# A four-layer Fourier and sliding-window attention kernel: pairs of visits regrouped, whid products spread over the rounds, twelve norms moved to the second spectral half

## The chip, the core and the metric

The kernel runs on one core of a Trainium2 chip. The metric is the time of one execution on the device in microseconds (us). The engines are PE (TensorE, matmuls and transposes), DVE (VectorE), ACT (ScalarE), POOL (GpSimd) and SP (SyncE), which here only issues DMAs. Each engine takes its instructions in order; what it waits for is a semaphore of another engine or of a DMA.

## What is computed

Four layers run one behind the other on x of 2048 rows and 640 columns. Layers 1 and 3 are Fourier mixing, layers 2 and 4 attention with 32 heads of 20 columns, in which a row sees itself and the 255 rows before it:

```python
def A(x):                      # dft matrices are inputs
    a = einsum("bsd,ed->bse", x, dft_hid_re)
    b = einsum("bsd,ed->bse", x, dft_hid_im)
    return einsum("ts,bse->bte", dft_seq_re, a) - einsum("ts,bse->bte", dft_seq_im, b)
def B(x):                      # H = 32, Dh = 20, W = 256
    q, k, v = heads(x @ wqkv)
    p = softmax(where(0 <= i - j < W, q @ k.T * Dh ** -0.5, -1e9))
    return rows(p @ v) @ wo
x = x + A(layernorm(x)); x = x + B(layernorm(x))
x = x + A(layernorm(x)); x = x + B(layernorm(x))
```

All is float32 to the outside.

## The kernel before

Numbers are split into two float16 parts, high and low, and a product is three matmuls: high by high, high by low, low by high. The program is four functions in a row: `spectral(0)`, `attention(0)`, `spectral(1)`, `attention(1)`.

**A spectral half.** The 16 row tiles of 128 rows are taken in four rounds of four tiles. For each tile, `Hidden.stage` multiplies the normed and transposed tile by the hidden DFT matrix (called whid here): four products of 15 matmuls of 320 columns. ACT and DVE drain each product from its bank of PSUM (lines 265 and 268) and make the seven operands `zc` of a Strassen-like scheme; a bank `f` is one of two. A round then takes eight steps j; a step makes seven sequence products of 12 matmuls each (`main_a`, `main_b`, `main_c`), for two output tiles. Its operands `cc` come from a block of the sequence DFT matrix: POOL makes four sums `cs` (lines 489 to 492), ACT the high parts (497), DVE the low parts (500). DVE adds the results to `res` or `pf` (523), POOL some of them on. Calls of `tick` give out the low parts and the steps of side work: the norm of a coming tile (`side_norm`), the transposes of a tile (`turn_x`), in the first half also the maxima and the splitting of wqkv. The whid products of the next round stand so: tiles 0 and 1 of the round behind steps 6 and 7 of the round before, tiles 2 and 3 between the rounds. In this part a scheduler orders each engine from the program's order.

In `spectral(1)` the tiles come normed, split and transposed out of DRAM: `attention(0)` norms its output tiles (`next_norm`), stores them as `xud`, and `Hidden.fetch` loads them with a transposing DMA.

**An attention half.** The order on each engine is that of the program. It runs over visits G. A visit takes four heads at one row tile; two visits, for the two row tiles of a block of 256 rows, make a pair n. A visit makes the scores of its heads (tiles `st`, first half), DVE masks them and takes row maxima (lines 1061, 1062); after the second visit of a pair the maxima are written as two float16 rows, `tops` (1068, 1069). `hand` transposes them on PE (`hand_on`) and ACT copies them into the operand of the scores (1083, two copies). Visits later `by_key` makes the scores again by key with the maximum subtracted, ACT takes the exponential (1110), POOL masks (1114, 1116), `values` multiplies by v, `back` turns the result and divides. The lags in visits are the constants `HAND_LAG`, `KEY_LAG`, `VALUE_LAG` and `BACK_LAG`. Each visit also runs a unit of other products (`run_unit`: 15 matmuls of q, k, v, of the output or of the next whid stage), and in some even visits a second. DVE's and ACT's own side work, norms and the splitting of wo, runs as `slow_step`, two steps per visit. The products, `values`, `back` and `hand` share the two banks `f`; line 346 drains a product of q or k.

All loads and stores go through SP's queue in order.

## Time and profile before

| | us |
|---|---|
| median of three runs | 2261.99 (2258.68 to 2270.58) |
| profiled execution, its own time | 2264.98 |
| its span | 2263.2 |
| PE busy | 2082.2 (92% of the span) |
| DVE, ACT, POOL busy | 1655.2, 1243.3, 1387.2 |
| mean granted clock of PE | 0.988 |

A busy share is of the whole span; the stages differ. On the trace, spectral 0 runs from 0 to about 593 us (the first scores of attention 0), attention 0 to about 1192, spectral 1 to about 1700, attention 1 to the end. Line 118 is the helper that issues every matmul, so PE's rows are told apart by their tiles. A wait stands as "who, line <- releaser, line: us in total, times, longest".

### The profile page before, as it was taken

What the parts mean: (1) busy time and instruction counts of PE and PEld (TensorE: products, weight loads), DVE (VectorE), ACT (ScalarE), POOL (GpSimd) and SP (SyncE); (2) the same over time, 40 slices, a digit from 0 to 9 for tenths busy, and PEclk for the clock granted to TensorE, in tenths of its full rate; (3) what the DMA queues carried; (4) which work ended last, traced back from release to release, by engine and by line L of the source; (5) the groups of instructions that cost most, each with busy time, mean ns of one, the idle gap of its engine ahead of it and who ended that gap; (6) DMA issues with size and microseconds to landing.
All of it is one profiled execution on the core that took longest, in us unless ns stands there. A gap on an engine that the chain in (4) does not pass through costs nothing.

```text
span 2263.2 us, 54344 instructions
## 1 busy us (share of the span) xinstructions
PE 2082.2 (92%) x21529; PEld 1484.5 (66%) x21529; DVE 1655.2 (73%) x3509; ACT 1243.3 (55%) x2087; POOL 1387.2 (61%) x1788
## 2 busy tenths in 40 slices
PE   7989899899889899999799999999998899999998
PEld 5767566667566666666556777777675666666665
DVE  7887858766668887887767758485857777777774
ACT  5434455344466767676554433433435677676764
POOL 5775968758355665556456858585764555556542
PEclk9999999999999999999899999999999999999999
DMA  6664636454534534354525546363743533443332
GB/s 248 224 213 141 231 133 221 159 197 162 133 86 98 119 85 95 83 113 97 150 83 177 180 138 209 108 210 119 278 137 85 108 81 80 106 96 80 83 78 54
DMA packets 274516, 309.96 MB, mean 137 GB/s; under 512 B 102868, under 2 KB 209620, under 8 KB 264916
## 3 DMA queue, kind: packets, MB, share of 16 engines
q1 hardware_dynamic: 273684, 305.82, 46.8%
q8 instruction: 169, 2.77, 0.5%
q14 instruction: 87, 0.71, 0.1%
q10 hardware_dynamic: 576, 0.66, 0.1%
HBM read 197.26 MB, written 86.87 MB: 126 GB/s over the span
## 4 chain that ended last, share of the span: by engine, by line
PE 43%; DVE 19%; ACT 9%; issue 5%; DMA 4%; POOL 1%; SPq 1%; DVEq 0%; ACTq 0%; POOLq 0%
PE pf L118 22%; PE y L118 7%; DVE m L1062 6%; PE z L118 5%; PE x L118 4%; PE st L118 4%; ACT ptq L1110 4%; ACT qs L1083 3%; DVE st L1061 3%; DVE tops L1069 1%; DVE cc L500 1%; DVE tops L1068 1%; DVE lnt L143 1%; DVE lnst L131 1%; DMA res<-accd 1%
## 5 line engine op out<-in xcount | busy, mean ns | idle before, releaser
L118 PEld LDWEIGHTS <-cc 128*128 128x128 f16 x5376 | 525.4, 98 | 213.3 <-issue 11.4
L1110 ACT ACTIVATE ptq<-st,shift,alpha 128x768 f32<-128x768 f32 (+2 forms) x512 | 474.2, 949 | 147.1 <-POOL ptq L1114 52.6
L118 PEld LDWEIGHTS <-big 128*128 128x128 f16 x4320 | 419.5, 99 | 177.3 <-issue 71.4
L1062 DVE TENSOR_REDUCE m<-st 128x2 f32<-128x512 f32 (+1 forms) x512 | 342.9, 671 | 8.8
L1061 DVE COPY_PREDICATED st<-mask,st 128x256 f32<-128x256 int32 x448 | 191.1, 427 | 184.0 <-PE st L118 145.5
L118 PE MATMUL pf<-early,big 128*128 128x256 f16 x2400 | 291.0, 274 | 18.5 <-ACT qs L1083 7.4
L497 ACT ACTIVATE cc<-cs 128x512 f16<-128x512 f32 x256 | 151.6, 623 | 254.6 <-POOL cs L489 125.4
L118 PE MATMUL y<-zc,cc 128*128 128x320 f16 x1728 | 263.8, 300 | 2.4 <-DVE pf L523 2.4
L500 DVE SCALAR_TENSOR_TENSOR cc<-cs,cc 128x512 f16<-128x512 f32 x256 | 254.3, 1009 | 12.9 <-ACT cc L497 12.7
L118 PE MATMUL pf<-big 128*128 128x320 f16 x1680 | 242.7, 304 | 22.3 <-DVE zc L268 9.6
L1114 POOL TENSOR_SCALAR_AFFINE_SELECT ptq<-ptq 128x512 f32<-128x512 f32 x224 | 144.8, 646 | 134.8 <-ACT ptq L1110 134.2
L1161 POOL CAST os<-o 128x160 f16<-128x160 f32 x128 | 40.5, 316 | 278.1 <-DVE o L1159 278.1
L1116 POOL TENSOR_SCALAR_AFFINE_SELECT ptq<-ptq 128x512 f32<-128x512 f32 x256 | 162.9, 636 | 59.6 <-ACT ptq L1110 59.6
L500 DVE SCALAR_TENSOR_TENSOR cc<-cq,cc 128x512 f16<-128x512 f32 x192 | 194.3, 1012 | 0.0
L118 PE MATMUL pf<-ptq,v 128*32 128x128 f32 (+1 forms) x3840 | 187.5, 335 | 1.4 <-POOL ptq L1116 1.4
L118 PE MATMUL z<-zc,cc 128*128 128x320 f16 x1152 | 177.8, 299 | 3.6 <-DVE res L523 3.6
L118 PE MATMUL x<-zc,cc 128*128 128x320 f16 x1152 | 179.4, 299 | 0.0
L118 PE MATMUL st<-ks,qs 62*128 62x128 f16 (+1 forms) x2016 | 133.1, 236 | 36.2 <-ACT ptq L1110 21.7
L1083 ACT ACTIVATE qs<-pf 2x512 f16<-2x512 f16 x224 | 130.7, 583 | 56.7 <-PE pf L118 54.1
L118 PEld LDWEIGHTS pf<-ptq,v 128*32 128x32 f32 x3840 | 108.2, 111 | 59.8 <-POOL ptq L1116 4.1
L118 PE MATMUL pf<-big,early 128*128 128x320 f16 x960 | 141.1, 299 | 5.9 <-ACT qs L1083 3.2
L118 PEld LDWEIGHTS <-qs 62*128 62x128 f16 x2016 | 82.1, 94 | 83.1 <-issue 64.6
(136 smaller groups left out, 3485.4 us busy)
## 6 DMA issues: line engine op xcount, KB each, us to landing
cq<-in_cmat_dram SPq DMA_DIRECT2D x64, 1024.0 KB
accd<-res SPq DMA_DIRECT2D x96, 320.0 KB
res<-accd SPq DMA_DIRECT2D x96, 320.0 KB
x<-x2d SPq DMA_DIRECT2D x64, 320.0 KB
qkd<-early SPq DMA_DIRECT2D x160, 128.0 KB
ks<-qkd SPq DMA_DIRECT2D x108, 160.0 KB
qs<-qkd SPq DMA_DIRECT2D x84, 160.0 KB
x2d<-res SPq DMA_DIRECT2D x32, 320.0 KB
```

The costliest lines, as they stand in the source:

```text
L118: i = getattr(nc.tensor, what)(*args, **kw)
L131: nc.vector.bn_stats(st[:, h], x[:, h * 320:(h + 1) * 320])
L143: ts(u, g, g, h, op0=OP.mult, op1=OP.mult)
L497: nc.scalar.activation(cc[m][:, 0], f, AF.Copy, scale=C_UP)
L500: nc.vector.scalar_tensor_tensor(cc[m][:, 1], f, C_UP, cc[m][:, 0], op0=OP.mult, op1=OP.subtract)
L1061: nc.vector.copy_predicated(sp[:, :, 2 * P:3 * P], mask[:, None, :].to_broadcast([P, 2, P]), far)
L1062: topped[0] = nc.vector.tensor_reduce(TOP[n][:, 2 * k:2 * k + 2, pi], sp[:, :, c0:3 * P], axis=AX.X, op=OP.max).ins
L1083: nc.scalar.activation(o, handed[n][rs].rearrange("r (i p) t -> r i p t", i=2), AF.Copy)
L1110: nc.scalar.activation(o[:, pi], tps[pi][:, :, first * P:3 * P], AF.Sigmoid, bias=shift, scale=alpha[:, 0:1])
L1114: nc.gpsimd.affine_select(out=q[:, :, a0], in_=q[:, :, a0], pattern=[[0, 4], [-1, P]], base=0, channel_multiplier=1, compare_op=OP.is_gt, ...
L1116: ins = nc.gpsimd.affine_select(out=q[:, :, a0 + 2], in_=q[:, :, a0 + 2], pattern=[[0, 4], [1, P]], base=0, channel_multiplier=-1, compare ...
L1161: nc.gpsimd.tensor_copy(hi, o)
```

## The change

- **Pairs of visits.** The four lags rise by one. The tops of a pair are still written in its second, odd visit; `hand` now runs in the even visit behind it, inside that visit's unit, after eight of its 15 matmuls (`HAND_AT`). `values` falls into the even visit too, `back` into the odd one, and the second unit is taken in odd visits. There is one more visit in all.
- **Side work of attention.** One step in odd visits, two in even ones; two lists, of which the second (`idle`: splitting of wo, norms for the next layer) is served when the first is empty. Rows for the next blocks are loaded two visits earlier and normed three visits earlier.
- **Norms.** Only tiles 0 to 3 of layer three are normed in `attention(0)`. The other twelve are normed in `spectral(1)` as in `spectral(0)`, with the scaling on ACT, and transposed by DMA from SBUF.
- **Whid products.** The table `STAGES` places the four tiles of the next round behind steps 2, 4, 5, 6 in round 0 and 1, 3, 5, 6 in rounds 1 and 2; nothing stands between the rounds. `zc` gets six buffers instead of four; the room comes from a third row of `pf` that is dropped (`p1` is overwritten instead of a new `u3`) and from a smaller area for DMA descriptors.
- **Residuals.** In the last round those of step 7 are loaded ahead of the first stacks of attention. The splitting of wo uses the buffers `res1` instead of `res0`.

```diff
-HAND_LAG = 1
-KEY_LAG = 3
-VALUE_LAG = 5
-BACK_LAG = 6
+HAND_LAG = 2
+KEY_LAG = 4
+VALUE_LAG = 6
+BACK_LAG = 7
+HAND_AT = 8
-NORM_STEPS = (4, 10)
+NORM_STEPS = (0, 4)
+STAGES = ((2, 4, 5, 6), (1, 3, 5, 6), (1, 3, 5, 6))
...
+                    if not first:
+                        turn_load(xt, xs.rearrange("p a b -> p (a b)"))
+                        yield 1
+                        return
...
-                add(u3, z, p1)
-                nc.gpsimd.tensor_tensor(x1[:, hi], x1[:, hi], u3, op=OP.add)
+                add(p1, z, p1)
+                nc.gpsimd.tensor_tensor(x1[:, hi], x1[:, hi], p1, op=OP.add)
...
+            def starts(k):
+                return [max(NJ * r + STAGES[r][k] - 3, k) for r in range(NR - 1)]
...
-                for k in range(0 if r == 0 else 2, RS):
+                for k in range(RS if r == 0 else 0):
...
                         for _ in early_qk:
                             pass
+                        RES[r, j] = load_res(r, j)
...
-                    if first:
-                        if r < NR - 1 and j in (3, 4):
-                            side.append(side_norm(RS * (r + 1) + j - 3))
-                        if r < NR - 1 and j == 5:
-                            turn_x(RS * (r + 1))
+                    for k in range(RS):
+                        if n in starts(k):
+                            side.append(side_norm(RS * (starts(k).index(n) + 1) + k))
+                    if r < NR - 1 and j == STAGES[r][0] - 1:
+                        turn_x(RS * (r + 1), 4 if first else 2)
...
-                    if r < NR - 1 and j >= NJ - 2:
-                        k = j - (NJ - 2)
+                    if r < NR - 1 and j in STAGES[r]:
+                        k = STAGES[r].index(j)
                         s = RS * (r + 1) + k
-                        if first:
-                            turned_x(s)
-                            turn_x(s + 1, 2 if k == 0 else 0)
-                            side.append(side_norm(s + 2))
-                        else:
-                            hidden.fetch(s)
+                        turned_x(s)
+                        if k < RS - 1:
+                            turn_x(s + 1, 2)
                         z_stage(s)
...
-                slow.append(next_norm(i, x3))
+                if i < RS:
+                    idle.append(next_norm(i, x3))
+                else:
+                    done[i, 2] = now[0]
...
-            def run_unit():
+            def run_unit(amid=None):
                 n = 0
                 while n < 15:
+                    if n >= HAND_AT and amid:
+                        amid()
+                        amid = None
...
-                for _ in range(2):
+                for _ in range(1 if G % 2 else 2):
                     slow_step()
...
-                if kept is not None:
-                    hand(kept)
-                    kept = None
                 credit[0] += 2 * max(rate, 400)
-                filled = run_unit()
-                if filled and credit[0] > SECOND and G % 2 == 0:
+                n = due(G, HAND_LAG)
+                run_unit(None if n is None else partial(hand, n))
+                if credit[0] > SECOND and G % 2:
                     run_unit()
-                n = due(G, HAND_LAG)
-                if n is not None:
-                    if filled:
-                        hand(n)
-                    else:
-                        kept = n
```

On PE in the middle of attention 0, from `values` (the `ptq,v` rows) over a unit (`early,big`) and the transposes of the maxima (`idh,tops`) to the next scores (`st<-ks,qs`); "..." leaves out more of the same pairs. Before:

```order
L118 MATMUL pf<-ptq,v 32x128 x4
L118 LDWEIGHTS big
L118 MATMUL pf<-early,big 128x256
...
L118 LDWEIGHTS tops_78
L118 MATMUL pf<-idh,tops_78 66x128
...
L118 LDWEIGHTS qs
L118 MATMUL st_6966<-ks,qs 128x256
```

and with the change:

```order
L120 MATMUL pf<-ptq,v 32x128 x4
L120 LDWEIGHTS big
L120 MATMUL pf<-early,big 128x256
...
L120 LDWEIGHTS tops_78
L120 MATMUL pf<-idh,tops_78 66x128
...
L120 LDWEIGHTS big
L120 MATMUL pf<-early,big 128x256
...
L120 LDWEIGHTS qs
L120 MATMUL st_6966<-ks,qs 128x128
```

The transposes moved from the end of the unit into it, and one visit further from the maxima they read.

On DVE in the first steps of spectral 1 (`cc` rows are low parts, `pf` and `res` rows the additions), before:

```order
L523 SCALAR_TENSOR_TENSOR pf<-y,pf 128x320
L500 SCALAR_TENSOR_TENSOR cc<-cq,cc 128x512
L523 SCALAR_TENSOR_TENSOR res<-x,res 128x320
L500 SCALAR_TENSOR_TENSOR cc<-cq,cc 128x512
L523 SCALAR_TENSOR_TENSOR res<-z,res 128x320
L500 SCALAR_TENSOR_TENSOR cc<-cs,cc 128x512
L523 SCALAR_TENSOR_TENSOR pf<-y,pf 128x320
L500 SCALAR_TENSOR_TENSOR cc<-cs,cc 128x512 x2
L523 SCALAR_TENSOR_TENSOR res<-z,res 128x320
```

and with the change:

```order
L529 SCALAR_TENSOR_TENSOR res<-z,res 128x320
L506 SCALAR_TENSOR_TENSOR cc<-cs,cc 128x512
L133 BN_STATS lnst<-xin 128x6
L529 SCALAR_TENSOR_TENSOR pf<-y,pf 128x320
L506 SCALAR_TENSOR_TENSOR cc<-cs,cc 128x512
L133 BN_STATS lnst<-xin 128x6
L506 SCALAR_TENSOR_TENSOR cc<-cs,cc 128x512
L136 BN_AGGR lnmv<-lnst 128x2
L142 TENSOR_SCALAR lnt<-lnmv 128x1
L143 TENSOR_SCALAR lnt<-lnt 128x1
L145 TENSOR_SCALAR lnt<-lnt 128x1
L146 TENSOR_SCALAR lnt<-lnt 128x1
```

The instructions of a tile's norm (statistics, then short scalars) stand between the low parts and the additions, where none stood.

On SP at the end of spectral 0, around the first stacks `ks` of attention and the residuals of the last step, tiles 125 and 126. Before:

```order
L178 DMA x2d_90<-res 128x640
L178 DMA ks<-onesd_165 2x4096
L178 DMA ks<-qkd_1_148 20x16x256 x6
L178 DMA ks<-onesd_164 2x4096 x2
L178 DMA ks<-qkd_0_147 20x16x256 x6
L178 DMA res<-accd_125 128x640
L178 DMA res<-accd_126 128x640
```

and with the change:

```order
L180 DMA x2d_90<-res 128x640
L180 DMA res<-accd_125 128x640
L180 DMA ks<-onesd_165 2x4096
L180 DMA res<-accd_126 128x640
L180 DMA ks<-qkd_1_148 20x16x256 x6
L180 DMA ks<-onesd_164 2x4096 x2
L180 DMA ks<-qkd_0_147 20x16x256 x6
```

The two residual loads moved ahead of nearly all of the stack loads.

More of the change, by code (lines that the diff above doesn't have):

```diff
@@ L886, in out_tile @@
                     yield from next_layer(i, x3)
-            slow, later = deque(), []
+            slow, idle, later = deque(), deque(), []
             def new_xs():
@@ L912, in split_wo @@
             def split_wo():
-                fs = [keep.tile([P, D], F32, tag="res0", name="wst", bufs=2) for n in range(2)]
+                fs = [keep.tile([P, D], F32, tag="res1", name="wst", bufs=2) for n in range(2)]
                 for n in range(2):
@@ L1195, in slow_step @@
                 with tc.issue_after(topped[0]):
-                    while slow:
-                        try:
-                            return next(slow[0])
-                        except StopIteration:
-                            slow.popleft()
+                    for line in (slow, idle):
+                        while line:
+                            try:
+                                return next(line[0])
+                            except StopIteration:
+                                line.popleft()
             queue_v(0)
@@ L1207, in attention @@
             if layer == 0:
-                slow.append(split_wo())
+                idle.append(split_wo())
             def due(G, lag):
```

21 lines of the change are left out of this document (13 added, 8 removed).

## Prediction

> **What bounds the kernel now.** I read the page's busy shares first, then the busy time by stretch, then who PE (TensorE) waits for in each stretch, and last the timeline at the longest waits. The page:
>
> ```profile
> PE 2082.2 (92%) x21529; PEld 1484.5 (66%) x21529; DVE 1655.2 (73%) x3509; ACT 1243.3 (55%) x2087; POOL 1387.2 (61%) x1788
> ```
>
> By stretch: spectral 0 without its start, the middle of attention 0, spectral 1, the middle of attention 1 (columns: window, length, busy us of PE, PEld, DVE, ACT, POOL with counts, granted clock, DMA share, GB/s):
>
> ```profile
> 120.00:600.00 480.00, 443.49 (x3293) 317.75 (x3291) 346.27 (x642) 210.11 (x400) 338.30 (x292) 0.98 0.55 180
> 600.00:1100.00 500.00, 448.12 (x6046) 319.45 (x6048) 390.38 (x963) 346.50 (x524) 277.66 (x504) 0.99 0.42 97
> 1185.00:1590.00 405.00, 401.58 (x2949) 288.02 (x2949) 278.67 (x454) 166.07 (x339) 282.30 (x233) 1.00 0.50 164
> 1700.00:2190.00 490.00, 450.12 (x6107) 322.43 (x6104) 362.40 (x861) 338.61 (x513) 263.45 (x495) 1.00 0.40 88
> ```
>
> PE bounds every stretch, and the change leaves its instructions as many as they were: 35475 rows in both programs. So only PE's idle time and its clock can give anything. Idle are 36.5, 51.9, 3.4 and 39.9 us in the four; spectral 1 has nothing left to gain. What PE waits for (us in total, times, longest), in spectral 0:
>
> ```profile
> PE pf L118 <- DVE zc L268: 8.3, 4, 5.3
> PE pf L118 <- DVE early L268: 8.2, 2, 6.2
> PE pf L118 <- POOL xs L170: 7.3, 4, 3.2
> PE pf L118 <- DVE big L268: 3.5, 1, 3.5
> ```
>
> in the middle of attention 0:
>
> ```profile
> PE pf L118 <- DVE tops L1069: 15.8, 15, 3.8
> PE pf L118 <- ACT qf L346: 6.6, 11, 0.8
> PE pf L118 <- ACT qs L1083: 6.1, 16, 0.6
> PE st L118 <- DVE m L1062: 2.9, 15, 0.2
> PE pf L118 <- ACT ks L1083: 2.3, 5, 0.5
> ```
>
> and in the middle of attention 1:
>
> ```profile
> PE pf L118 <- DVE tops L1069: 7.3, 12, 1.2
> PE pf L118 <- ACT qs L1083: 6.3, 21, 0.6
> PE pf L118 <- ACT qf L346: 5.8, 10, 0.8
> PE pf L118 <- ACT ks L1083: 2.3, 5, 0.5
> ```
>
> L268 drains a whid product's bank; L1069 and L1083 are the two halves of handing the score maxima on.
>
> **Part 1: whid products spread over the rounds.** All three long drains of spectral 0 (near 140, 283 and 424 us) stand at the first whid product set inside a round. The middle one, with the load ahead of it, the clock behind it, and the same load in spectral 1:
>
> ```profile
> 283.08 4.16 PE L118 MATMUL pf<-big 128*128 128x320 f16 x15 [6.19 <-DVE early L268]
> ```
>
> ```profile
> 240.00:280.00 40.00, 33.70 (x243) 23.78 (x242) 35.51 (x52) 18.52 (x32) 38.88 (x27) 0.96 0.72 242
> 283.00:288.00 5.00, 4.92 (x22) 3.07 (x22) 1.25 (x5) 1.09 (x3) 3.52 (x4) 0.50 0.13 54
> 1220.00:1280.00 60.00, 60.00 (x444) 43.23 (x442) 49.54 (x68) 23.35 (x44) 50.30 (x38) 1.00 0.58 199
> 1320.00:1340.00 20.00, 20.00 (x149) 14.38 (x148) 8.21 (x18) 11.21 (x25) 8.31 (x10) 1.00 0.32 71
> ```
>
> Ahead of the stall POOL is busy 38.9 of 40 us, DVE 35.5: the steps of a round without whid products load both beyond what they can hold, and the drain arrives late. While spectral 1 does whid products (last row) DVE and POOL need 8.2 and 8.3 of 20 us. Putting one set after a step in the middle of the round lets both catch up four times instead of once. The waits named are 8.3 + 8.2 + 3.5 = 20.0 at drains and about 5 of the 7.3 at transposes; 0.02 of clock over 480 us is 10 us more (0.50 right behind the stall). A set still ends on the same in-order ACT and DVE, now four times inside a round, so I take a little over half: 14 us of waits and 5 of clock, **-19**. Bounds: 0 (each new place stalls as the old one did) and -35.
>
> The Trainium skill, "TensorE: Matmul & The Clock Gate", section "What's actually happening", says an idle window of about 3.4 us halves PE's clock until about 3.4 us of work have passed. The 0.50 agrees; by its figures four such gaps are worth an estimated 7 us.
>
> **Part 2: heads and values in one visit.** Now the maxima of a pair of visits are finished on DVE at the end of the odd visit, and PE transposes them at that same visit's end. One pair of attention 1:
>
> ```profile
> 1890.45 0.66 PE L118 MATMUL st<-ks,qs 62*128 62x128 f16 x8
> 1891.52 0.43 DVE L1061 COPY_PREDICATED st<-mask,st 128x256 f32<-128x256 int32 x1 [0.94 <-PE st L118]
> 1894.47 0.55 DVE L1069 SCALAR_TENSOR_TENSOR tops<-m,tops 128x8 f16<-128x8 f32 x1
> 1895.08 0.41 PE L118 MATMUL pf<-idh,tops 128*66 128x128 f16 x4
> 1898.89 0.66 PE L118 MATMUL st<-ks,qs 62*128 62x128 f16 x8
> ```
>
> From the first mask to the last maximum DVE needs 3.5 us; PE has just enough to do meanwhile, and waits when its product is a short one. After the change the transposes come a visit later, behind eight matmuls of the next product: over 3 us more slack. So the waits on tops go: -7 of 7.3 in attention 1 and -15 of 15.8 in attention 0. Of these, 5.9 stand at its start, where splits of wo lie ahead of tops on DVE; only two of five do after the change, and none ahead of the first tops:
>
> ```profile
> 600.26 0.41 PE L118 MATMUL pf<-idh,tops 128*66 128x128 f16 x4 [2.05 <-DVE tops L1069]
> 609.42 0.64 PE L118 MATMUL pf<-idh,tops 128*66 128x128 f16 x4 [3.83 <-DVE tops L1069]
> ```
>
> The waits for a bank (qf, qs, ks: 15.0 and 14.4 us) come from the head's copies on ACT ending after the next product wants their bank. The transposes now run seven matmuls (about 0.9 us) before the end of their product, and these waits are 0.4 to 0.6 us each: I take half, -7.5 and -7, since ACT keeps its amount of work.
>
> Costs: tops now lie on DVE between an odd visit's maxima and those of the even one, ahead of the next scores: 1.15 us more ahead of the visit with values, which PE fills with 4.6 us (1890.45 to 1895.08). Waits of 0.2 us on maxima exist already; I add 2 us per attention (0 to 8). And there is one more visit in each attention, a visit of the tail. Its price, by starts of visits in the tail (keys, then next keys):
>
> ```profile
> 2236.54 0.51 PE L118 MATMUL st<-qs,ks 62*128 62x128 f16 x12
> 2240.01 0.51 PE L118 MATMUL st<-qs,ks 62*128 62x128 f16 x12
> 2244.67 0.51 PE L118 MATMUL st<-qs,ks 62*128 62x128 f16 x12
> ```
>
> Those take 3.5 and 4.7 us with a product and values in them; one with keys alone is nearer its two exponentials, so +2.5 (0 if leftover products fill it, to 4.7).
>
> **Part 3: twelve of sixteen norms of layer two move from attention 0 to spectral 1.** One tile in attention 0:
>
> ```profile
> L131 DVE BATCH_NORM_STATS2 lnst<-x 128x6 f32<-128x320 f32 x42 | 18.5, 478 | 0.0
> L143 DVE TENSOR_SCALAR lnt<-lnt 128x1 f32<-128x1 f32 x63 | 17.0, 272 | 2.0
> L158 DVE TENSOR_SCALAR lny<-x,lnmv,lnt 128x640 f32<-128x640 f32 x21 | 16.7, 813 | 0.0
> L144 DVE TENSOR_SCALAR lnt<-lnt 128x1 f32<-128x1 f32 x63 | 13.3, 212 | 1.7
> L170 POOL TENSOR_TENSOR xs<-lny,xs 128x640 f16<-128x640 f32 x21 | 29.4, 1398 | 11.9 <-ACT xs L169 11.9
> ```
>
> DVE: 2 x 0.48 + 3 x (0.27 + 0.21) + 0.81 + about 0.5 of small ones = 3.7 us, times 12 = 45 us off a DVE that is busy 390 of 500. It is not the bound, so this only loosens PE's order: -2 (0 to -10). In spectral 1 each costs DVE about 3.1 us (its scaling goes to ACT, two passes there), POOL 1.4 as before: DVE rises from 279 to about 316 of 405 us, POOL to 299. PE covers it if it is even. In the first three steps it is not: a step is 84 matmuls, 11.4 us, DVE needs 49.5 / 60 x 11.4 = 9.4 of it and gets a norm in each, 12.5. It falls 1 us behind per step until the first whid set, which gives back 4. On SP, twelve stores of xud leave attention 0; loads of x and transposes that wait for POOL's xs stand in spectral 1 ahead of cq and res loads, which run a step ahead. I put **+4** on all this (0 to 15).
>
> **Part 4: last residuals ahead of the stacks.** They are issued behind 16 stack loads at the end of a spectral half. The chain of waits, and the longest of PE's three waits behind it:
>
> ```profile
> 581.25 8.06 DMA res<-accd
> ```
>
> ```profile
> PE z L118 <- DVE res L523: 0.9, 1, 0.9
> ```
>
> The three are about 2 us, in spectral 1 less: -3 in all (0 to -5). Reusing p1 instead of u3 changes no time: it is the same operation on another row.
>
> **Sum.** Spectral 0 -19; attention 0 -15 - 7.5 - 2 + 2 + 2.5 = -20; attention 1 -7 - 7 + 2 + 2.5 = -9.5; residuals -3; spectral 1 +4: -47.5. The profiled execution took 2264.98 us (span 2263.2): 2217.5. It lies 3.0 above the median 2261.99, so I say **2217**.
>
> **Rivals.** A: the forecast, 2217 (2195 to 2240), 0.61. B: the waits move. The transposes stop waiting, but scores then wait for maxima behind tops, and the new whid places stall half as much as the old: spectral 0 -8, attentions -6 and -2, residuals -3, spectral 1 +4: 2250. For it: DVE is at 78% in attention 0 and runs in order. Against: per pair the change gives DVE less. 0.18. C, slower: spectral 1 loses its full PE. Place: the first two whid sets of its three rounds; point: DVE need above the step, 12.5 against 11.4, before a set. Price as in spectral 0, where a first set cost 20.0 / 3 = 6.7 us of wait and 2 of clock (15 matmuls in 4.16 us at 0.50): 6 x 8.7 = 52 instead of 4, and with spectral 0's gain gone too, 2217 + 48 + 19 = 2284. Against: spectral 1 has no splitting of wqkv, and POOL has 50 of 60 there. 0.10. D: all named waits and all of the clock loss go: spectral 0 -35, attention 0 -31, attention 1 -22, residuals -5: 2172. 0.09. E: the change doesn't do what it says; but the two programs' orders do differ at all these places: 0.02, 2262.
>
> Beside C: the Trainium skill, "SBUF — State Buffer", section "SBUF: two separate sides", has DVE instructions with two SBUF inputs and POOL's take turns on one port pair. The splits moved would then block DVE for 12 x 1.4 = 17 us more, an estimate. No row here separates that.
>
> **Numbers.** Half a per cent, 11 us, is about what a measurement tells from no change. Faster: A, D and half of B, 0.79. Same: the other half of B and E, 0.11. Slower: C, 0.10. Range 2188 to 2256: all of A, most of B, some of D.
>
> **What would show it.** Part 1: PE's waits on L268 and xs in spectral 0 below 12 us, no stretch at clock 0.50. Part 2: waits on tops near 0 in both attentions, qs and qf halved, DVE m below 6. Part 3: PE idle in spectral 1 below 8 us. I would be wrong if spectral 1 is longer by over 15 us, or if attention 1, which only part 2 touches, doesn't shorten.

## The result and the profile after

| | before | after |
|---|---|---|
| median, the two compared on the same chip | 2262.85 us (2258.68 to 2270.58) | 2212.41 us (2207.26 to 2213.61) |
| ratio, 95% interval | | 0.977 (0.974 to 0.980) |
| profiled execution, own time; span | 2264.98; 2263.2 | 2207.26; 2205.2 |

The forecast was 2217, the range 2188 to 2256. The total came within 5 us of the forecast, but hardly one of its terms did. The first line of the page after, busy time by engine:

```profile
PE 2050.6 (93%) x21529; PEld 1477.5 (67%) x21529; DVE 1610.1 (73%) x3509; ACT 1250.6 (57%) x2099; POOL 1375.1 (62%) x1788
```

PE has as many instructions as before, and is busy for 31.6 us less. The prediction had said that only idle time and the clock could give anything. PE's idle time (span less busy) fell from 181.0 to 154.6, by 26.4; the mean granted clock rose from 0.988 to 0.994, which is worth about 0.006 x 2263 = 14 us of busy time. Some 18 us of busy time are left that the clock doesn't explain.

The stages, cut at the first scores of each attention half and at the first sequence product of spectral 1, from the timeline's rows:

| stage | before | after | difference | forecast |
|---|---|---|---|---|
| spectral 0 | 593.1 | 577.4 | -15.8 | -19, and most of the residuals' -3 |
| attention 0 | 618.4 | 582.7 | -35.7 | -20 |
| spectral 1 | 488.1 | 498.3 | +10.2 | +4 |
| attention 1 | 560.1 | 543.3 | -16.8 | -9.5 |

They are those of one execution each. After's was the fastest of its four, 5 us below their median, so its stages are a little short. Three of the four stages by stretch, after (window, length, busy us of PE, PEld, DVE, ACT, POOL, clock, DMA share, GB/s):

```profile
40.00:577.00 537.00, 512.30 (x3834) 369.82 (x3833) 391.35 (x750) 238.58 (x462) 391.70 (x341) 0.99 0.55 191
577.00:1160.00 583.00, 530.30 (x7087) 381.73 (x7085) 431.57 (x1039) 404.53 (x622) 317.44 (x567) 0.99 0.44 105
1658.00:2202.00 544.00, 496.68 (x6834) 357.96 (x6832) 398.21 (x950) 378.74 (x568) 288.55 (x540) 0.99 0.40 87
```

and the two attention halves before, over the whole stage, which the prediction had only in part:

```profile
593.00:1211.00 618.00, 547.79 (x7079) 385.56 (x7079) 473.76 (x1182) 410.06 (x632) 333.03 (x586) 0.98 0.43 104
1700.00:2260.00 560.00, 507.87 (x6830) 360.01 (x6827) 402.65 (x950) 376.64 (x567) 287.42 (x540) 0.99 0.38 84
```

In attention 1, which of the change sees only the pairing and the side work, PE's busy time falls by 11.2 us, 1.3 of it by the clock (three stretches of 3.4 us at half clock before, two after); idle is 52.1 before, 47.3 after. So most of what this stage gained stands in no row of waits.

What PE waits for after, in spectral 0 (to 560 us; us in total, times, longest):

```profile
PE pf L120 <- DVE zc L270: 10.3, 5, 3.5
PE pf L120 <- DVE early L270: 5.8, 2, 4.4
PE pf L120 <- POOL xs L172: 4.1, 3, 1.9
PE pf L120 <- ACT xs L171: 2.6, 1, 2.6
```

The four rows of before (in the prediction, which end on the same drains and transposes) were 27.3; these are 22.8. The new places of the whid products stall nearly as much as the old ones, one long enough to halve the clock (0.50 from 253 to 257.5 us):

```profile
252.83 4.16 PE L120 MATMUL pf<-big 128*128 128x320 f16 x15 [4.39 <-DVE early L270]
```

In the whole of attention 1, after:

```profile
PE st L120 <- ACT ptq L1131: 16.8, 32, 2.0
PE pf L120 <- ACT pvs L1163: 7.3, 17, 0.7
PE pf L120 <- DVE m L1083: 6.5, 6, 1.4
PE pf L120 <- DVE lnt L143: 4.8, 5, 1.4
```

The waits on tops, qf and qs are gone or below 1.5 us, as forecast (here 7.3, 5.8 and 6.8 before). But PE now waits for `pvs`, the copy that empties the bank of values, and longer for the exponentials `ptq` (0.9 and 13.4 before).

In spectral 1 the stall stands where part 3 had put it, at the first whid set of round 0:

```profile
1197.21 5.91 PE L120 MATMUL pf<-big 128*128 128x320 f16 x30 [3.61 <-DVE zc L270]
```

### The profile page after: what moved, and what is told of

The parts are those of the page before. It is cut to its first block, busy times and chain, and to the rows that moved or that the text cites. A ratio compares the mean times of both kernels' runs of the same rounds, so it can differ in the third digit from the quotient of the medians.

```text
span 2205.2 us, 54413 instructions
## 1 busy us (share of the span) xinstructions
PE 2050.6 (93%) x21529; PEld 1477.5 (67%) x21529; DVE 1610.1 (73%) x3509; ACT 1250.6 (57%) x2099; POOL 1375.1 (62%) x1788
## 4 chain that ended last, share of the span: by engine, by line
PE 54%; DVE 26%; ACT 10%; issue 5%; DMA 2%; POOL 2%; SPq 0%; DVEq 0%; ACTq 0%; POOLq 0%
PE pf L120 24%; PE y L120 11%; PE x L120 7%; PE z L120 7%; DVE m L1083 6%; PE st L120 5%; DVE cc L506 5%; DVE st L1082 4%; ACT ptq L1131 4%; ACT qs L1104 2%; DVE lnt L145 1%; DVE tops L1089 1%; DVE tops L1090 1%; DVE lnst L133 1%; ACT qf L348 1%
## 5 line engine op out<-in xcount | busy, mean ns | idle before, releaser
L1131 ACT ACTIVATE ptq<-st,shift,alpha 128x768 f32<-128x768 f32 (+2 forms) x512 | 482.2, 950 | 201.3 <-PE st L120 75.5
L120 PEld LDWEIGHTS <-big 128*128 128x128 f16 x4320 | 415.1, 98 | 154.9 <-issue 51.4
L120 PE MATMUL pf<-early,big 128*128 128x256 f16 x2400 | 298.4, 273 | 0.9 <-DVE o L1180 0.7
L120 PE MATMUL pf<-big 128*128 128x320 f16 x1680 | 242.3, 302 | 29.3 <-DVE zc L270 16.7
L506 DVE SCALAR_TENSOR_TENSOR cc<-cs,cc 128x512 f16<-128x512 f32 x256 | 229.5, 903 | 0.0
L570 POOL TENSOR_TENSOR res<-res,pf 128x320 f32<-128x320 f32 x64 | 78.0, 1219 | 138.7 <-DVE pf L529 123.2
L1104 ACT ACTIVATE qs<-pf 2x512 f16<-2x512 f16 x224 | 131.4, 587 | 47.6 <-PE pf L120 46.1
L120 PE MATMUL pf<-big,early 128*128 128x320 f16 x960 | 146.1, 299 | 0.4 <-ACT v L839 0.4
```

Of the source, the lines that this page charges most:

```text
L120: i = getattr(nc.tensor, what)(*args, **kw)
L506: nc.vector.scalar_tensor_tensor(cc[m][:, 1], f, C_UP, cc[m][:, 0], op0=OP.mult, op1=OP.subtract)
L570: nc.gpsimd.tensor_tensor(x1[:, hi], x1[:, hi], p1, op=OP.add)
L1104: nc.scalar.activation(o, handed[n][rs].rearrange("r (i p) t -> r i p t", i=2), AF.Copy)
L1131: nc.scalar.activation(o[:, pi], tps[pi][:, :, first * P:3 * P], AF.Sigmoid, bias=shift, scale=alpha[:, 0:1])
```

## The experiments

None of the twelve kernels changes what is computed. The first eight take the changed kernel and undo a part or shift a count; the next three add one part alone to the kernel before; the last looks for something better. In their edits lines are shortened or joined, and "..." leaves lines out. The two lists of side work and the earlier loading of rows were not undone by themselves. All kernels by stage (length, and for the attention halves PE's busy and idle time in it, from the windows of one execution):

| kernel | median | spectral 0 | attention 0 = busy + idle | spectral 1 | attention 1 = busy + idle |
|---|---|---|---|---|---|
| before | 2262.85 | 593.1 | 618.4 = 548.3 + 70.1 | 488.1 | 560.1 = 508.2 + 51.9 |
| after | 2212.41 | 577.4 | 582.7 = 530.0 + 52.7 | 498.3 | 543.3 = 496.3 + 47.0 |
| norms back, two steps | 2231.60 | 577.3 | 605.6 = 536.2 + 69.4 | 488.2 | 552.8 = 501.1 + 51.6 |
| whid placed as before | 2220.36 | 584.9 | 582.5 = 529.6 + 52.9 | 498.6 | 545.4 = 499.1 + 46.3 |
| hand as before | 2246.48 | 578.6 | 602.3 = 546.7 + 55.6 | 499.3 | 561.0 = 509.0 + 52.0 |
| residuals as before | 2222.60 | 583.4 | 582.1 = 529.2 + 52.9 | 506.7 | 543.6 = 497.7 + 45.9 |
| two steps in each visit | 2221.89 | 577.4 | 591.0 = 533.7 + 57.3 | 499.6 | 550.5 = 499.7 + 50.8 |
| norms back, steps kept | 2220.46 | 577.2 | 597.9 = 535.1 + 62.8 | 488.0 | 551.5 = 501.7 + 49.8 |
| hand after 12 matmuls | 2209.87 | 576.7 | 582.5 = 538.1 + 44.4 | 498.9 | 542.5 = 500.8 + 41.7 |
| steps swapped | 2228.63 | 578.0 | 590.5 = 529.9 + 60.6 | 500.2 | 553.3 = 498.8 + 54.5 |
| before + residuals | 2256.40 | 586.4 | 616.4 = 546.6 + 69.8 | 486.7 | 560.8 = 510.6 + 50.2 |
| before + hand | 2251.25 | 590.0 | 610.9 = 535.5 + 75.4 | 488.1 | 556.0 = 501.2 + 54.8 |
| before + whid | 2260.30 | 583.5 | 620.0 = 550.7 + 69.3 | 490.0 | 558.5 = 508.0 + 50.5 |
| two norms back, hand after 12 | 2206.36 | 578.1 | 582.9 = 536.8 + 46.1 | 494.4 | 545.1 = 503.8 + 41.3 |

How far a single execution can be trusted is seen where the program of a stage is the same: attention 0 of before, of "before + residuals" and of "before + whid" took 618.4, 616.4 and 620.0, spectral 1 488.1, 486.7 and 490.0. Stage differences below 3 us are not read. One stage went further astray: attention 1 of experiment 6, whose program there is that of after, took 8.2 us more. Medians come from different chips, each time with before beside the kernel; before's medians were 2262.6 to 2264.2 us.

### 1. Norms back in attention 0, with two steps per visit

```diff
-                if i < RS: idle.append(next_norm(i, x3))
-                else: done[i, 2] = now[0]
+                slow.append(next_norm(i, x3))
...
+                    if not first: hidden.fetch(s); yield 1; return    # in turn_x
...
-                for _ in range(1 if G % 2 else 2):
+                for _ in range(2):
```

> The changed kernel with all sixteen norms of layer three back in attention 0 (two steps of side work per visit, stored as xud and fetched by a transposing DMA as before). The two profiles differ by -16 us in spectral 0, -35 in attention 0, +7 in spectral 1 and -14 in attention 1. Theory of the prediction (norms are off the path, the pairing of visits gives nearly all of attention 0): attention 0 lengthens by at most 6 us, spectral 1 gets its 7 us back, the whole lies at 2207 to 2214 us. Rival (the 21 us that attention 0 gained over attention 1 belong to the twelve norms, above all in its last block): attention 0 lengthens by 15 to 22 us, spectral 1 shortens by 5 to 7, the whole lies at 2221 to 2229 us.

Measured 2231.60 (ratio 0.986, 0.983 to 0.989): 19 us above after, beyond even what the rival allowed. Spectral 1 gave 10.1 us back, attention 0 took 22.9. But two things were changed, the norms and the count of steps, so 5 and 6 split them.

### 2. Whid products placed as before in spectral 0

```diff
-                for k in range(RS if r == 0 else 0):
+                for k in range(0 if r == 0 else 2 if first else RS, RS):
...
+                    if first and r < NR - 1 and j >= NJ - 2:
+                        ... turned_x(s); turn_x(s + 1, ...); side.append(side_norm(s + 2)); z_stage(s)
```

> The changed kernel with the whid products of spectral 0 alone in their old places (two sets in steps 6 and 7, two between the rounds); spectral 1 as changed. Theory of the prediction (POOL and DVE are full when the first set comes): spectral 0 lengthens by 13 to 17 us, half-clock stretches come back, the whole lies at 2225 to 2230 us. Rival (spectral 0 gained by the residuals and by the smaller DMA area or the larger zc, not by the places): spectral 0 lengthens by less than 5 us, the whole stays at 2212 to 2217 us.

Measured 2220.36 (0.981, 0.978 to 0.984); spectral 0 is 7.5 us longer, no other stage by 3. That lies between the two: the part gives something, and less than half of the forecast.

### 3. The hand as before

```diff
-HAND_LAG, KEY_LAG, VALUE_LAG, BACK_LAG = 2, 4, 6, 7
+HAND_LAG, KEY_LAG, VALUE_LAG, BACK_LAG = 1, 3, 5, 6
...
-                run_unit(None if n is None else partial(hand, n))
-                if credit[0] > SECOND and G % 2:
+                filled = run_unit()
+                if filled and credit[0] > SECOND and G % 2 == 0:
                     run_unit()
...
+                if n is not None:       # hand(n) behind the unit, or kept for the next visit
```

> The changed kernel with the old lags and the old place of the heads (transposes at the end of the odd visit, second product in even visits), norms and all else as changed. Theory of the prediction (the pairing carries both attentions): attention 0 lengthens by 22 us or more, attention 1 by 12 to 15, the whole lies at 2246 to 2252 us. Rival (norms carry the larger part of attention 0): attention 0 lengthens by 12 to 15 us, as attention 1 does, the whole lies at 2236 to 2242 us.

Measured 2246.48 (0.992, 0.990 to 0.995): 34 us are lost, the least that the theory allowed. By stage it is 19.6 in attention 0, short of its 22, and 17.7 in attention 1, above its 12 to 15; the rival's 12 to 15 in both is out. The waits of before come back in attention 0:

```profile
PE pf L120 <- DVE tops L1090: 14.4, 23, 1.6
PE pf L120 <- ACT qf L348: 6.1, 10, 0.8
PE pf L120 <- ACT qs L1104: 5.3, 13, 0.6
```

Yet idle time grows by only 2.9 us there, since the waits for pvs go and those for ptq fall from 14.9 to 4.9 us. It is busy time that grows, by 16.7 us.

### 4. The last step's residuals behind the stacks

```diff
-                        RES[r, j] = load_res(r, j)
```

> The changed kernel with the last residuals loaded at their old place, behind the stack loads. Theory of the prediction: 2 us longer at the end of spectral 0 and 1 at the end of spectral 1, the whole at 2214 to 2217 us. Rival (the stack loads end the spectral half anyway): no difference beyond 1 us in either half.

Measured 2222.60 (0.982, 0.979 to 0.985), 10 us above after where 2 to 5 were expected: spectral 0 is 6.0 us longer, spectral 1 8.4. The waits behind it, at the end of both:

```profile
576.38 2.71 PE L120 MATMUL z<-zc,cc 128*128 128x320 f16 x12 [3.48 <-DVE res L529]
578.87 2.60 PE L120 MATMUL y<-zc,cc 128*128 128x320 f16 x12
581.31 2.20 PE L120 MATMUL pf<-big,early 128*128 128x320 f16 x15
1664.57 3.36 PE L120 MATMUL z<-zc,cc 128*128 128x320 f16 x12 [5.85 <-DVE res L529]
```

Twelve such matmuls take 1.79 us at full clock; here 2.71 and 3.36. The one wait costs a gap of 3.5 to 5.9 us and then up to 1.6 us of slower clock. Before, PE stood there for only 0.9 us, and its rows at the end of spectral 0 show why:

```profile
585.98 1.79 PE L118 MATMUL y<-zc,cc 128*128 128x320 f16 x12 [0.58 <-DVE pf L523]
587.61 2.20 PE L118 MATMUL pf<-big,early 128*128 128x320 f16 x15
590.75 1.79 PE L118 MATMUL z<-zc,cc 128*128 128x320 f16 x12 [0.94 <-DVE res L523]
```

In before a product y and a unit of 15 matmuls, 3.8 us, stand ahead of the product z whose addition needs the residual; in this kernel, as in after, they stand behind it. The loads are as late in both: z starts 9.5 us after they were issued before, and 8.3 here. So this edit brings back the old place of the loads, but not the old order on PE.

### 5. Two steps of side work in each visit

```diff
-                for _ in range(1 if G % 2 else 2):
+                for _ in range(2):
```

> The changed kernel with two steps of side work in every visit instead of two in even and one in odd visits. In the run with the norms back, attention 1 was 9.5 us longer than in the changed kernel, and only these steps differ there. Theory (a second step in the odd visit, behind heads and back, delays DVE's maxima and so the next scores): attention 1 and attention 0 each 7 to 10 us longer, the whole at 2226 to 2232 us. Rival (the 9.5 us came with the norms or the chip, not with the steps): both attentions within 2 us of the changed kernel, the whole at 2210 to 2216 us.

Measured 2221.89 (0.981, 0.980 to 0.983): 9.5 us lost, which lies between the rival's range and the theory's; by stage it is 8.3 in attention 0 and 7.2 in attention 1, as the theory had them. An edit of one number, which the prediction hadn't priced, is worth as much as the pairing alone (10).

### 6. Norms back in attention 0, steps as in the change

The edit of 1 without its last two lines.

> All sixteen norms of layer three back in attention 0, but with the changed kernel's three steps per pair of visits. Theory (of the 22.9 us that attention 0 lost with the norms back, about 9 were the steps): attention 0 longer by 12 to 15 us, spectral 1 shorter by 10, attention 1 unchanged, the whole at 2213 to 2218 us. Rival (the norms themselves cost all of it): attention 0 longer by 20 us or more, the whole at 2221 to 2226 us. Theory of the prediction (2 us for the norms): attention 0 longer by at most 6 us, the whole below 2209 us.

Measured 2220.46 (0.981, 0.979 to 0.983): 8 us lost, between the theory's range and the rival's; the theory of the prediction is out. Attention 0 is 15.2 us longer, of that 10.1 of idle time; spectral 1 is 10.3 shorter and has before's length. PE's waits in attention 0, first this kernel, then after:

```profile
PE st L120 <- ACT ptq L1128: 22.5, 31, 2.6
PE pf L120 <- ACT pvs L1160: 16.5, 29, 1.1
```

```profile
PE st L120 <- ACT ptq L1131: 14.9, 30, 2.0
PE pf L120 <- ACT pvs L1163: 12.1, 22, 1.4
```

The norms on DVE, which is not the bound, delay what ACT and then PE wait for. Attention 1 is 8.2 us longer here, although its program is after's: 2.8 of idle time and 5.4 of busy time. In it are two waits for a load of scores' operands, of which after has none above 0.5 us in this stage, and six stretches of 3.4 us at half clock instead of two:

```profile
PE st L120 <- DMA qs<-qkd: 5.2, 2, 3.0
```

So that stage's difference is the execution's, not the edit's, and those of 1 and 8 in attention 1, with one such wait each (3.1 and 3.3 us), may hold some of it; 5 has none.

### 7. The hand after twelve matmuls of the unit

```diff
-HAND_AT = 8
+HAND_AT = 12
```

> The changed kernel with the heads' transposes after twelve of fifteen matmuls instead of eight, half a microsecond later. In the changed kernel PE waits there for the copy of the values' bank (pvs): 11.3 us in the middle of attention 0 and 7.0 in attention 1. Theory (these waits are late by less than 0.7 us and are covered by four more matmuls): pvs waits below half, each attention 3 to 8 us shorter, the whole at 2199 to 2207 us. Rival (the slack is conserved: the heads' copies end later by as much, and the next product waits for its bank, qs, as in the kernel before): no attention differs by more than 2 us, waits on qs come back, the whole at 2210 to 2216 us.

Measured 2209.87 (0.976, 0.974 to 0.977): no stage moves by 1 us, as the rival had it. In attention 1 the waits for pvs are gone and those for the head's copies are back:

```profile
PE pf L120 <- ACT qs L1104: 10.2, 28, 1.1
PE st L120 <- ACT ptq L1131: 9.1, 12, 2.0
PE pf L120 <- ACT ks L1104: 4.2, 7, 1.9
```

Idle falls by 5.3 us, busy rises by 4.5. Eight or twelve makes no difference to the time: what PE doesn't wait at one place it loses at another.

### 8. Two steps in odd visits, one in even ones

```diff
-                for _ in range(1 if G % 2 else 2):
+                for _ in range(2 if G % 2 else 1):
```

> The changed kernel with its three steps of side work per pair turned round: two in odd visits, one in even ones. Theory (the place matters, since DVE's odd visit already holds tops and the division of back): both attentions 5 to 9 us longer, the whole at 2221 to 2230 us. Rival (only the number of steps per pair matters): both within 2 us, the whole at 2210 to 2216 us.

Measured 2228.63 (0.984, 0.983 to 0.986), 16 us above after with the same number of steps per pair, and 7 above two steps everywhere; attention 0 is 7.8 us longer, attention 1 10.0. In attention 1 (from 1690 to 2150 us, where after has 6.6):

```profile
PE pf L120 <- ACT pvs L1163: 21.4, 23, 1.7
```

So what counts is not only how much side work there is but in which visit it stands. In the order of DVE the steps of an odd visit lie ahead of the masks and maxima of the even one, which holds the values.

### 9. Before, with the residuals ahead of the stacks

```diff
+                        RES[r, j] = load_res(r, j)     # behind early_qk, ahead of the stacks
...
-                fs = [keep.tile([P, D], F32, tag="res0", name="wst", bufs=2) for n in range(2)]
+                fs = [keep.tile([P, D], F32, tag="res1", name="wst", bufs=2) for n in range(2)]
```

> The kernel before with part 4 alone: the last step's two residuals are loaded ahead of the sixteen stack loads in both spectral halves. Nothing that is computed changes. Undoing this part in the changed kernel cost 6.1 us in spectral 0 and 8.4 us in spectral 1. Theory: the price of the late residual depends on how late PE is at that place for other reasons; in the kernel before PE waited only 0.9 us there, so the part alone gives 0 to 4 us in all: 2258 to 2263 us. Rival: it is worth what undoing it cost, whatever the rest: about 14 us, 2246 to 2251 us.

Measured 2256.40 (0.998, 0.997 to 1.000): 4 us, with an interval from 0.5 to 8. The median is just below the theory's figures, and the rival is out. The stage's 6.7 us overstate it: the programs are equal up to the last step, and at the third long stall the two executions already stood 4.4 us apart, first before, then this kernel:

```profile
424.34 4.16 PE L118 MATMUL pf<-big 128*128 128x320 f16 x15 [5.27 <-DVE zc L268]
```

```profile
419.96 3.87 PE L118 MATMUL pf<-big 128*128 128x320 f16 x15 [5.27 <-DVE zc L268]
```

From there to the first scores they take 168.8 and 166.5 us: 2.3 for the edit. In this kernel, too, PE's order at that place is that of the change, z ahead of y and the unit; the waits of before there (0.6, 0.9 and 0.6 us) are gone.

### 10. Before, with the hand of the change

The reverse of 3, put into the kernel before; two steps per visit stay. The hand runs in even visits, as in the change.

> The kernel before with part 2 alone: heads handed on inside the unit of an odd visit, lags 2, 4, 6 and 7; two steps of side work per visit stay, and the sixteen norms stay in attention 0. Nothing that is computed changes. Theory: part 2 was under-sized by my terms, and alone it is worth nearly what undoing it cost (19.6 us in attention 0, 17.7 in attention 1): attention 1 shorter by 14 to 19, attention 0 by 12 to 20, 2224 to 2236 us. Rival: my terms (18 and 9.5 us) were right, and undoing cost more because the changed kernel has less slack elsewhere: attention 1 shorter by 7 to 11, 2234 to 2242 us. If the norms and the second step of side work stand in its way in attention 0, then that stage alone gains less than 12.

Measured 2251.25 (0.996, 0.995 to 0.998): 9 us faster by the ratio, and neither theory had it so little: attention 0 gains 7.5 us, attention 1 only 4.1. In attention 1:

```profile
PE st L119 <- ACT ptq L1116: 16.2, 31, 2.0
PE pf L119 <- ACT pvs L1148: 16.2, 20, 1.5
PE pf L119 <- DVE m L1068: 9.7, 5, 2.1
```

The waits on tops, qf and qs that the forecast counted are gone or below 2 us, and idle time has *risen*, from 51.9 to 54.8 (in attention 0 from 70.1 to 75.4): the waits have moved to pvs, ptq and m. What makes the kernel faster all the same is busy time, 7.0 us less in attention 1 and 12.8 in attention 0. ACT's exponentials in this kernel, and in after (middle of attention 1):

```profile
L1116 ACT ACTIVATE ptq<-st,shift,alpha 128x768 f32<-128x768 f32 x196 | 193.5, 990 | 78.3 <-DVE m L1068 30.7 <-PE st L119 22.9 <-DVE tops L1075 11.9
```

```profile
L1131 ACT ACTIVATE ptq<-st,shift,alpha 128x768 f32<-128x768 f32 x199 | 196.0, 991 | 74.7 <-DVE m L1083 25.3 <-PE st L120 24.5 <-DVE tops L1090 12.8
```

Ahead of an exponential ACT waits 30.7 us for maxima here and 25.3 in after, and the copy to pvs stands behind the exponential on ACT. That fits 5 and 8: one step less on DVE in the odd visit lets the maxima, the exponentials and then the bank of values come earlier. That the step acts by this road is argued from the order and these rows; that it acts is shown by 5 and 8.

### 11. Before, with the whid products of spectral 0 spread

```diff
+STAGES = ((2, 4, 5, 6), (1, 3, 5, 6), (1, 3, 5, 6))
...
-                for k in range(0 if r == 0 else 2, RS):
+                for k in range(0 if r == 0 else RS if first else 2, RS):
...
+                    if first and r < NR - 1 and j in STAGES[r]: ...
```

> The kernel before with part 1 alone: whid products, norms and transposes of spectral 0 spread over its rounds; spectral 1 still takes its tiles from attention 0. It includes the two whid buffers more and the row less that the change makes for this. Nothing that is computed changes. Theory: the new places stall as well, only less, and spectral 0 gains what undoing this part cost: 6 to 9 us, 2253 to 2257 us. Rival: my term of 19 us, with the loss in the changed kernel hidden by something else: spectral 0 shorter by 15 to 22 us, 2241 to 2247 us.

Measured 2260.30 (0.999, 0.998 to 1.000): -4 to +1 us, less than either theory said. Spectral 0 of the profiled execution is 9.6 shorter than before's, but before's is the longest of the three whose program is the same there but for the residuals at its end (593.1, 590.0 in 10, 586.4 in 9). Forward the part is worth some 2 us, undone (2) it cost 8; both are far from 19.

### 12. Tiles 4 and 5 normed in attention 0, hand after twelve

```diff
-                if i < RS:
+                if i < RS + 2:
...
-                        if n in starts(k):
+                        if n in starts(k) and (first or n > 1):
...
+                    if not first and s < RS + 2: hidden.fetch(s); yield 1; return    # in turn_x
```

> The changed kernel with the norms of tiles 4 and 5 of the last layer moved back into attention 0 (as idle work, behind the others) and fetched in spectral 1, and with the transposes of a head placed behind twelve matmuls of the unit instead of eight, which by itself changed no stage by over 1 us. Nothing that is computed changes. Theory: spectral 1's ten extra us come from norms in its first steps, which load DVE beyond a step until the first whid set; with two of them gone the wait of 3.6 us at that set and its clock go, so spectral 1 is shorter by 4 to 7 us, attention 0 longer by 1 to 3: 2204 to 2209 us. Rival: the ten us are spread over all rounds, two of twelve norms give back 2 us and attention 0 takes 2.5: 2209 to 2213 us.

Measured 2206.36 (0.977, 0.975 to 0.978). Spectral 1 is 4.5 us shorter than in 7, attention 0 unchanged, as the theory had it, and the wait that part 3 named is down to 1.07 us, with a full clock behind it:

```profile
1195.69 4.24 PE L120 MATMUL pf<-big 128*128 128x320 f16 x30 [1.07 <-DVE zc L270]
```

The kernel's ratio to before is not told apart from that of the change (0.977) or of 7 (0.976), so none of them is a better version that this study could show.

## Why the prediction was right, and where it was not

**The likeliest case held in the total, by errors that cancel, and that is luck.** In the profiled executions the forecast was 23 us short in the two attention halves and 12 us too high in what the spectral halves gain. It also stayed with the profiled execution, 3 us above the median; from the median the same sum gives 2214.5. Its parts were tried from both ends (us by which the kernel changes; for the undone parts, by which it gets longer):

| part | forecast | alone, added to before | undone in after |
|---|---|---|---|
| 1 whid spread in spectral 0 | -19 | -2 | 8 |
| 2 heads and values in one visit | -27.5 | -9 | 34 |
| 3 norms moved | +2 | not tried | 8 |
| side steps in odd visits | none | not tried | 9.5 |
| 4 residuals | -3 | -4 | 10 |

Added alone, 1, 2 and 4 give 15 us of the 50; undone one by one, all give 70. The parts depend on one another, so neither column is "the" price.

**Part 1 was over-sized.** The step that failed is "putting one set after a step in the middle of the round lets both catch up". The waits on its lines fell from 27.3 to 22.8, not below 12, and a stretch at clock 0.50 is still there; ahead of it, from 248 to 253 us, DVE is busy for 4.57 of 5 us, so it has not caught up. The clock's share was sized about right: six stretches of 3.4 us at half clock in spectral 0 became three (four with part 1 alone, 11), some 5 us. The bound "each new place stalls as the old one did" was nearer than the middle that was taken.

**Part 2: the sign right, the reason half wrong.** The waits on tops, qf and qs went, even beyond the half that was counted. But the rule "only PE's idle time and its clock can give anything" failed: alone, the part makes idle time longer. The gain is in how often PE breaks off. Gaps of more than 0.02 us between PE's rows, counted over the stages:

| | attention 0: gaps, idle us, busy us | attention 1 |
|---|---|---|
| before | 174, 69.4, 548.3 | 165, 51.0, 508.2 |
| hand as before (3) | 182, 55.2, 546.7 | 176, 51.7, 509.0 |
| before + hand (10) | 104, 74.4, 535.5 | 88, 54.1, 501.2 |
| after | 95, 51.4, 530.0 | 89, 45.5, 496.3 |
| hand after 12 (7) | 116, 43.5, 538.1 | 109, 40.3, 500.8 |

Where the hand is the old one there are 165 to 182 gaps, where it is the new one 88 to 116, and busy time goes with them. To take the clock out, count half of PE's busy time in the stretches at half clock as lost to it. What is left of busy time in attention 1 is 503 to 504 us in the four kernels with the old hand, 496 to 497 in the two with the hand after twelve matmuls, and 491 to 494 in the eight with it after eight: between before and after 0.14 us per gap ((11.9 - 1.3) / 76). The rows of one pair show how, before and after:

```profile
1895.08 0.41 PE L118 MATMUL pf<-idh,tops 128*66 128x128 f16 x4
1895.42 0.54 PE L118 MATMUL st<-ks,qs 62*128 62x256 f16 x9
...
1896.28 0.44 PE L118 MATMUL pf<-idf,pvs 128*128 128x128 f32 x2
1896.76 2.20 PE L118 MATMUL pf<-bo,ot 128*128 128x320 f16 x15
```

```profile
1837.84 0.38 PE L120 MATMUL pf<-idh,tops 128*66 128x128 f16 x4
1838.06 1.11 PE L120 MATMUL pf<-big,early 128*128 128x320 f16 x7
...
1839.88 0.44 PE L120 MATMUL pf<-idf,pvs 128*128 128x128 f32 x2
1840.15 2.20 PE L120 MATMUL pf<-bo,ot 128*128 128x320 f16 x15
```

The two transposes of pvs hold PE until the next start for 0.48 us before and 0.27 after. A row's time goes on while the next instruction already runs, unless that one has to wait; a break so costs its gap and the overlap. Counted over attention 1, the second of these transposes is followed by a gap in 58 of 64 pairs before and holds PE for 0.27 us in each; after, 58 of 64 have no gap and hold it for 0.12. That is 8.7 of the 10.6 us. The four of tops hold PE for 0.34 and 0.22 us, but not by a break: after, a product follows them and not scores. Those 6 us are taken back by the products, which are cut once more.

The same count shows why part 2 is worth 9 us alone and 34 undone:

| | idle | clock | rest of busy | length |
|---|---|---|---|---|
| added to before, attention 0 | +5.3 | -2.9 | -10.0 | -7.5 |
| added to before, attention 1 | +2.9 | +5.4 | -12.5 | -4.1 |
| undone in after, attention 0 | +2.9 | +5.2 | +11.5 | +19.6 |
| undone in after, attention 1 | +5.0 | +1.4 | +11.3 | +17.7 |

The breaks are worth 10 to 12.5 us per attention from either end. What differs is the idle time and the clock: alone, in attention 1, 8 of 12.5 us go back into longer waits (pvs, ptq, m) and into the clock; undone, both add to the loss. The forecast of 27.5 us lies between; its size came from counting the waits on tops as gained in full and those for a bank by half, and not from the breaks.

**Rival B** was thus true of part 2, though with another place than it named: the scores' waits on maxima (`st <- DVE m`) fell in attention 1 from 3.7 to 1.8 us, and the waits went to pvs, to ptq and, for a product, to m (6.5). B's price needed that nothing made room on DVE; the norms and the odd step did.

**Part 3 had the wrong sign.** "It is not the bound, so this only loosens PE's order: -2": putting the norms back costs attention 0 15 us, most of it idle time of PE (6). The medians say the same: the whole is 8 us longer although spectral 1 gives 10 back. So the term "-2 (0 to -10)" missed. An engine at 78% that runs in order, and for which ACT and PE wait in every visit, is not covered. In spectral 1 the +4 became +10.2, inside its bound of 15; place and mechanism were right (12), and the first whid set's stall is 4 to 5 us of it. Rival C, 52 us there, did not come: later sets stall for 0.9 to 1.4 us each.

**The count of steps was left out**, and is worth 9.5 us (5). The prediction saw the line in the diff, and gave it no term.

**Part 4 was priced from its wait in before**, 2 us, and is worth 2 to 4 there (9). Undone in after it costs 10 (4), because there PE's order has the waiting product ahead of 3.8 us of other work that covers the late load in before: the price is right for the kernel that was profiled, and not for the changed one.

**Of the signs that would show it**, tops near 0 and qf and qs halved came; waits on L268's successor below 12, no stretch at 0.50, waits on maxima below 6 and idle in spectral 1 below 8 (12.5) did not. Neither of the two things that were to refute it happened: spectral 1 is not longer by 15, and attention 1 got shorter.

## What to carry to other kernels

Count how often the bounding engine breaks off, and not only how long it waits: waits that a reordering removes can come back at the next place, while the busy time saved by fewer breaks stayed gained here from both ends. An engine below its limit whose results are awaited in every round is on the path; where its side work stands in the round (here one step, in the visit ahead of the one with the values) can weigh as much as a reordering of the main work. What a late load costs depends on how much other work the bounding engine's order has ahead of the instruction that needs it. A price read from a wait holds for the kernel in which it was read: try a part alone and undone before calling either the price.

## What the runs showed of the hardware

**Whether a gap of 2.6 us halves the clock depends on where it falls in a grid of 3.41 us.** The same 15 matmuls behind the same gap, in before and in 9, whose programs are equal there:

```profile
139.85 2.20 PE L118 MATMUL pf<-big 128*128 128x320 f16 x15 [2.61 <-DVE zc L268]
```

```profile
139.88 3.87 PE L118 MATMUL pf<-big 128*128 128x320 f16 x15 [2.62 <-DVE zc L268]
```

The granted clock from 140 to 144 us was 1.00 in the first and 0.57 in the second. In every trace of this case the stretches at half clock last 3.41 us or a multiple of it (but for the one cut off by the end of the program) and start on one grid of that step, which lies elsewhere in each execution. In 9 a window of the grid ends at 140.14 us and holds the whole gap; PE is busy for 23% of it, and the next window runs at half clock. In before the grid cuts the gap at 138.24 us; the two windows are busy for 71% and 53%, and the clock stays. Counted over the fourteen traces from 20 us after the first matmul on, windows at full clock in which PE was busy for less than 40% were followed by half clock in 89 of 90 cases, those from 40 to 60% in 53 of 295, and those above 60% in none of 8435. The Trainium skill, "TensorE: Matmul & The Clock Gate", section "What's actually happening", gives an idle window of about 3.4 us as what throttles; here a window with 0.8 us of work in it was enough.

The slower matmuls cost nothing at this place: the next wait for a bank is 0.57 us in 9 and 3.49 in before, and 9 stands 1.2 us ahead behind it. So this is not what put equal programs 4 us apart at 424 us; the waits differ, and why they do stays open.

**A load that lands just in time makes a stage's time uncertain.** PE's waits for the scores' operands (`qs<-qkd`) in attention 1 came to 5.2 us in 6 and to 0.3 in after, and the program of that stage is the same in both.
